# Retention on one core: the query-state product cut into four 64 by 64 quarters, with every second head pair swapped

## The chip, the cores and the metric

The kernel runs on one core of a Trainium2 chip. The metric is the device time of one launch in microseconds. The core has a matrix engine (PE; its weight loads are listed apart as PEld), a vector engine (DVE), a scalar engine (ACT), GpSimd (POOL) and a queue engine (SP) that issues most DMAs. Engines run their own instruction streams in order and meet at semaphores.

## The reference, cut to what matters

```python
scores = scale * np.matmul(q, k.transpose(0, 1, 3, 2))          # B=8, H=8, S=576, D=64
gamma  = 1.0 - 2.0 ** (-5.0 - np.arange(H))
Dmat   = np.where(rel >= 0, gamma[:, None, None] ** rel, 0.0)   # rel = pos_i - pos_j
x      = np.matmul(scores * Dmat, v)                            # retention, (B*S, H*D) = 4608 x 512
logits = x @ w_gate + modality_bias[modality_id]                # 8 experts, one per token
x      = gate * (relu(x @ w1[e]) @ w2[e])                       # routed expert layer
out    = relu(x @ w_in) ** 2 @ w_out                            # dense layer, d_ff = 2048
```

The change touches the first step only, and of the second the product that yields the gate's logits.

## The kernel before, in words

The 4608 tokens go through three stages in one program: `phase0` (retention and routing), `phase12` (expert layers, and a conversion of the dense weights that runs beside them) and `phase3` (the dense layer). The program is written out in a fixed order, and each engine keeps it.

`phase0` works through 36 tiles t of 128 tokens. Since 576 tokens are four and a half tiles, a batch row starts at t % 9 = 0 and another in the middle of t % 9 = 4. The 512 channels are four chunks c of 128 partitions; a chunk holds two heads, head 2c on partitions 0 to 63 and head 2c+1 on 64 to 127. Retention is written as a recurrence: besides the scores inside the tile, a 64 by 64 state for each head (the sum over earlier tiles of key times decayed value) is multiplied with the tile's queries. Per round the program issues, in this order:

- `qk(t+1)`: line 488, scores of the next tile, 8 matmuls with 64 rows by 128 columns of weights, two heads at a time on the two halves of the array's rows, into PSUM banks 0 and 1; line 481 on POOL makes the decayed values `vh`; line 491 on DVE masks the scores into `at`.
- `om(t)`: line 508, the query-state product, 4 matmuls of 128 by 128, one for each chunk. Their weights are the tile `sbd`, in which a chunk's two 64 by 64 states stand on the diagonal of a 128 by 128 block; the other two quarters were set to zero at the start (lines 579 and 580) and stay so. Line 512 adds the scores times `vh`, 8 matmuls with 128 rows by 64 columns, even heads on the left half of the columns, odd heads on the right. All of it goes into bank 2. Line 517 on DVE multiplies it by the decay `odec` into `xt` (lines 520 and 521 where a batch row ends inside the tile). There is no state at t % 9 = 0, and at t % 9 = 4 it counts for 64 of the 128 tokens.
- `kv(t)`: line 536, the state's update in bank 3, and line 542 on ACT, two copies of 64 partitions into the other `sbd`.
- `xm(t-1)`: line 555, `xt` of the tile before times `iwg`, a matrix of the identity (which turns the tile round so that tokens are on partitions) and 8 columns of `w_gate`. The two results go to the banks 5, 6 and 7 in turn; lines 557 and 558 on ACT copy them out.

Routing (`route_a`, `route_b`, `route_c`) is cut into small steps, mostly on DVE, that `adv` sows among these rounds for each group of four tiles: softmax terms, a scaling of four tiles on ACT (lines 193 to 201), a store on SP (line 202), then two small bf16 matmuls (lines 209 and 210) whose result takes the next of the banks 5 to 7, and at last the table of tokens (line 246). The last group is done in one go, and its counts set which expert is gathered first: POOL reads the table (line 431) and issues the gathers (line 434).

Loads are issued on SP, a few at the start on ACT's queue. The program has eight semaphores for them, taken in turn; a DMA's issue waits until the DMA eight before it has landed.

Of the kernel before, what the change touches and what calls it, by code (L numbers as in the profile page):

```python
# [9 lines left out]
F32 = mybir.dt.float32  # L10
# [4 lines left out]
AF = mybir.ActivationFunctionType  # L15
ALU = mybir.AluOpType
# [4 lines left out]
B, H, S, D = 8, 8, 576, 64  # L21
NT, DM = B * S, H * D
NE, FE = 8, 1024
FF = 2048
P = 128
# [5 lines left out]
KD = DM // P  # L31
LC = P + NE
# [11 lines left out]
def consts():  # L44
    gamma = 1.0 - 2.0 ** (-5.0 - np.arange(H, dtype=np.float64))
    scale = 1.0 / np.sqrt(float(D))
    tok = np.arange(9 * P)
    pos = (tok % S).astype(np.float64)
    vdec = scale * gamma[None, :] ** (-(pos[:, None] + 1.0))
    vdec = vdec.reshape(9, P, H).transpose(1, 0, 2)  # L50
    p = np.arange(S, dtype=np.float64)
    od = gamma[:, None] ** (p[None, :] + 1.0)
    odec = np.repeat(od.reshape(KD, 2, 1, S), D, axis=2)
    odec = odec.reshape(KD, P, S).transpose(1, 0, 2)
    j = np.arange(P)
    causal = (j[:, None] <= j[None, :]).astype(np.float64)
    half = causal * ((j[:, None] < 64) == (j[None, :] < 64))
    ident = np.eye(P)
    tri = (j[:, None] < j[None, :]).astype(np.float64)
    ones = np.ones((P, P))  # L60
    m = np.concatenate([causal, half, ident, tri, ones], axis=1)
    rows = {}
    rows["iota"] = np.arange(KEYS, dtype=np.float64)
    rows["rev"] = 8.0 - np.arange(NE)
    rows["k512"] = 512.0 * np.arange(9)
    e = np.arange(NE)
    rows["le"] = (e[None, :] <= e[:, None]).astype(np.float64).reshape(-1)
    rows["eid"] = e
    rows["e36"] = DMAX * e
    s = np.arange(NS)  # L70
    rows["sv"] = np.where(s <= NF, s, s - 1)
    off, cat, o = {}, [], 0
    for k_, a in rows.items():
        off[k_] = (o, len(a))
        o += len(a)
        cat.append(a)
    r = np.repeat(np.concatenate(cat)[None, :], P, axis=0)
    ids = P * np.arange(NTILE)[None, :] + j[:, None] - IDOFF
    off["ids"] = (o, NTILE)
    r = np.concatenate([r, ids], axis=1)  # L80
    f = lambda a: np.ascontiguousarray(a, dtype=np.float32)
    return f(vdec), f(odec), f(m), f(r), off
# [6 lines left out]
def kernel(ctx, tc, qT, kT, kN, vN, modT, w_gate, mbias, w1, w2, w_in, w_out,  # L89
# [28 lines left out]

    psY = Banks(y0=[0], y1=[1], y2=[2], y3=[3], tps=[4])
    psG = Banks(g=[5, 6, 7])  # L120

    xd = dram.tile([NT, DM], F32, name="xd")
    yd = dram.tile([DM, NT + TS], F32, name="yd")
# [5 lines left out]
    ident = const.tile([P, P], F32, name="ident")  # L129
# [22 lines left out]
    G = 4  # L152
# [52 lines left out]
    def route_b(g, eng):  # L205
        t0 = G * g
        oh, pm = OH[g]
        ps = psG.tile([P, G, NE], F32, tag="g", name="psr")
        pe.matmul(ps, trib[:, 0, :], oh, start=True, stop=False, skip_group_check=True)
        pe.matmul(ps, trib[:, 1, :], acc[:, t0:t0 + G, :], start=False, stop=True, skip_group_check=True)  # L210
        yield
        rm = sm.tile([P, G, NE], F32, tag="rm", name="rm")
        rk = sm.tile([P, G], F32, tag="rk", name="rk")
        dd = sm.tile([P, G], F32, tag="dd", name="dd")
        bb = sm.tile([P, G], F32, tag="bb", name="bb")
        ky = sm.tile([P, G], F32, tag="ky", name="ky")
        dve.tensor_scalar(out=ky, in0=pm, scalar1=-float(DMAX), scalar2=float(NE * DMAX),
                          op0=ALU.mult, op1=ALU.add)
        dve.tensor_tensor(out=rm, in0=ps, in1=oh, op=ALU.mult)
        yield  # L220
        dve.tensor_reduce(out=rk, in_=rm, axis=AX.X, op=ALU.add)
        yield
        dve.tensor_scalar(out=dd, in0=rk, scalar1=-63.5, scalar2=1.0 / P, op0=ALU.add, op1=ALU.mult)
        yield
        dve.tensor_scalar(out=dd, in0=dd, scalar1=MAGIC, scalar2=-MAGIC, op0=ALU.add, op1=ALU.add)
        yield
        dve.tensor_tensor(out=ky, in0=ky, in1=dd, op=ALU.add)
        dve.scalar_tensor_tensor(out=bb, in0=dd, scalar=-float(P), in1=rk, op0=ALU.mult, op1=ALU.add)
        yield
        st = wp.tile([P, G * (P + KEYS)], F32R, tag="w", name="okb")  # L230
        ob = st[:, :G * P].rearrange("p (g b) -> p g b", g=G)
        ok = st[:, G * P:].rearrange("p (g b) -> p g b", g=G)
        ids = row("ids")
        RS[g] = (ob, ok)
        for j in range(G):
            eng.tensor_scalar(out=ob[:, j, :], in0=row("iota")[:, :P], scalar1=bb[:, j:j + 1],
                              scalar2=None, op0=ALU.is_equal)
            eng.tensor_scalar(out=ok[:, j, :], in0=row("iota"), scalar1=ky[:, j:j + 1],
                              scalar2=ids[:, t0 + j:t0 + j + 1], op0=ALU.is_equal, op1=ALU.mult)
            yield  # L240
# [8 lines left out]
        dve.tensor_scalar(out=tab, in0=tps, scalar1=IDOFF, scalar2=None, op0=ALU.add)  # L249

    def count(t, name):
        ps = psG.tile([P, NE], F32, tag="g", name=name)
        pe.matmul(ps, trib[:, 1, :], acc[:, t, :], start=True, stop=True, skip_group_check=True)
        return ps

# [182 lines left out]
    def phase0():  # L438
        with ExitStack() as c0:
# [9 lines left out]
            mb = cp.tile([P, 2, NE], F32, name="mb")  # L449
            modi = cp.tile([P, NTILE, 2], I32, name="modi")  # L450
            modf = cp.tile([P, 2, NTILE], F32, name="modf")
            sbd = [cp.tile([P, KD, P], F32, name=f"sbd{i}") for i in range(2)]
            sps = psY.tile([P, KD, D], F32, tag="y3", name="sps")

            U = {}
# [42 lines left out]
            def om(t):  # L498
                b_, a, vn, kn = U[t // 4]
                x = t % 4  # L500
                at, vh = AT[t], VH[t]
                ps = psY.tile([P, KD, P], F32, tag="y2", name="pso")
                tt = t % 9
                ns = 0 if tt == 0 else (64 if tt == 4 else P)
                sb = sbd[scur[0]]
                for c in range(KD):
                    if ns:
                        pe.matmul(ps[:, c, :ns], sb[:, c, :], a[:, c, x * P:x * P + ns],
                                  start=(c == 0), stop=False, skip_group_check=True)
                for c in range(KD):  # L510
                    for i in range(2):
                        pe.matmul(ps[64 * i:64 * i + 64, c, :], vh[:, 2 * c + i, :], at[:, KD * i + c, :],
                                  start=(c == 0 and not ns), stop=(c == KD - 1), skip_group_check=True)
                xt = wk.tile([P, KD, P], F32, tag="xt", name="xt")
                p0 = (t * P) % S
                if p0 + P <= S:
                    dve.tensor_tensor(out=xt, in0=ps, in1=odec[:, :, p0:p0 + P], op=ALU.mult)
                else:
                    n = S - p0
                    dve.tensor_tensor(out=xt[:, :, :n], in0=ps[:, :, :n], in1=odec[:, :, p0:S], op=ALU.mult)  # L520
                    dve.tensor_tensor(out=xt[:, :, n:], in0=ps[:, :, n:], in1=odec[:, :, 0:P - n], op=ALU.mult)
                XT[t] = xt

            def kv(t):
# [11 lines left out]
                        pe.matmul(sps[64 * i:64 * i + 64, c, :], kn[r0:, x, h * D:h * D + D], vh[r0:, h, :],  # L536
                                  start=(new and c == 0), stop=True, skip_group_check=True)
                scur[0] ^= 1
                sb = sbd[scur[0]]
                for i in range(2):  # L540
                    o = 64 * i
                    act.activation(sb[o:o + 64, :, o:o + 64], sps[o:o + 64, :, :], AF.Copy)

            def xm(t):
                g, j = t // G, t % G
# [3 lines left out]
                xt = XT.pop(t)  # L549
                xs = XS[g][:, j, :].rearrange("p (c d) -> p c d", c=KD)  # L550
                for a in range(2):
                    ps = psG.tile([P, 2, LC], F32, tag="g", name="psx")
                    for i in range(2):
                        c = 2 * a + i
                        pe.matmul(ps[:, i, :], xt[:, c, :], iwg[:, c, :], start=True, stop=True,
                                  skip_group_check=True)
                    act.activation(LP[g][:, j, 2 * a:2 * a + 2, :], ps[:, :, P:], AF.Copy)
                    act.activation(xs[:, 2 * a:2 * a + 2, :], ps[:, :, :P], AF.Copy)
# [7 lines left out]
            load(0, 0, 1, both, (2, 3))  # L566
            sp.dma_start(odec[:, :, 0:P], odec_d[:, :, 0:P])
            act.dma_start(ident, mats_d[:, 2 * P:3 * P])
            act.dma_start(iwg[:, :, P:], w_gate.rearrange("(c p) e -> p c e", p=P))
            load(0, 1, 1, both, (2, 3))  # L570
            load(0, 2, 2, parts=(0, 1))
            sp.dma_start(odec[:, :, P:256], odec_d[:, :, P:256])
# [3 lines left out]
            sp.dma_start(modi, modT.bitcast(I32).rearrange("p (t w) -> p t w", w=2))  # L576
            sp.dma_start(mb, mbias.unsqueeze(0).to_broadcast([P, 2, NE]))
            sp.dma_start(trio, mats_d[:, 3 * P:5 * P].rearrange("p (a b) -> p a b", a=2))
            dve.memset(sbd[0], 0.0)
            dve.memset(sbd[1], 0.0)  # L580
            dve.memset(acc[:, 0, :], 0.0)
            noadv = lambda n: None
            qk(0, noadv)
            for c in range(KD):
                pool.tensor_copy(iwg[:, c, :P], ident)
            alloc(1)
            load(1, 4, 4)

# [73 lines left out]
                        stage[t + 4] = lambda g=g: (adv(99), route_c(g))  # L662

    def phase12():
        with ExitStack() as c1:
            xp = c1.enter_context(tc.tile_pool(name="xp", bufs=2))
            hp = c1.enter_context(tc.tile_pool(name="hp", bufs=3))
# [693 lines left out]
```

## Time and profile before

| | |
|---|---|
| Three runs | 1436.12, 1429.42, 1434.08 us; median 1434.08 |
| Profiled execution | 1428.05 us, of which the span from first to last instruction is 1426.3 us |
| Busy over the span | PE 1358.7 us (95%), PEld 1251.9, DVE 1026.4 (72%), ACT 635.8 (45%), POOL 172.6 (12%) |
| `phase0` | 0 to about 194.6 us |
| Mean granted PE clock | 0.984 of full speed |

In a timeline a line is one or more like instructions in a row: start, length, engine, line, tiles, shape and count, and in brackets the idle time before it with what ended it. Each fp32 matmul of the program shows as two records, so the 4 matmuls of line 508 read x8 and the 8 of line 512 read x16. The length of a line of matmuls includes the tail of the last, so what a step costs is read from its start to the start of the next. Shapes of matmuls are given as rows by columns of the array.

### The profile page before, as it was taken

The page shows a single profiled execution, that of the slowest core. Times are in us where ns is not written, and L with a number is a line of the kernel's source. Part 1 is how long each engine was busy: PE and PEld are TensorE (multiplying, and loading weights), DVE is VectorE, ACT ScalarE, POOL GpSimd, SP SyncE. Part 2 cuts the span into 40 slices and gives each one's busy share as a digit, 9 for nine tenths or more (in the row PEclk, how much of TensorE's full clock was granted, in tenths as well). Part 3 has the DMA queues.
Part 4 walks back from the last instruction along what each step waited for, and adds up shares of the span by engine and source line. Part 5 has one row for each costly group of instructions (what it writes and reads, how often), then busy time and mean ns, then how long its engine had stood idle before and what let it go on. Part 6 is the DMA issues. An engine that isn't in the chain of part 4 may idle for free. (4 is left out here: it accounts for less than half of the span.)

```text
span 1426.3 us, 26456 instructions
## 1 busy us (share of the span) xinstructions
PE 1358.7 (95%) x10384; PEld 1251.9 (88%) x10384; DVE 1026.4 (72%) x2004; ACT 635.8 (45%) x1317; POOL 172.6 (12%) x164
## 2 busy tenths in 40 slices
PE   6999998999999999988899999999999999999985
PEld 6898877888788888878899999999999999999984
DVE  2677756887878878553888887767766777688764
ACT  1444543545354454443555555554434444334321
POOL 3222112101110110000211111100000000021112
PEclk9999999999999999998999999999999999999998
DMA  9978256888889888888644455477445564787672
GB/s 341 355 271 296 78 167 229 246 237 254 298 244 269 251 318 229 236 235 272 234 178 178 185 215 194 179 312 265 174 163 195 211 224 184 276 278 274 222 252 102
DMA packets 143733, 332.40 MB, mean 233 GB/s; under 512 B 20208, under 2 KB 54512, under 8 KB 143600
## 3 DMA queue, kind: packets, MB, share of 16 engines
q1 hardware_dynamic: 135520, 310.06, 64.9%
q0 software_dynamic: 5920, 19.40, 3.6%
q8 instruction: 83, 1.36, 0.4%
q10 hardware_dynamic: 2160, 1.17, 0.3%
q14 instruction: 50, 0.41, 0.1%
HBM read 222.57 MB, written 108.02 MB: 232 GB/s over the span
## 5 line engine op out<-in xcount | busy, mean ns | idle before, releaser
L1140 PE MATMUL bank<-w,h 128*128 128x256 f32 x1008 | 284.8, 283 | 9.4 <-DVE h L1241 9.4
L1138 PE MATMUL bank<-w,h 128*128 128x256 f32 x1008 | 283.9, 282 | 7.8 <-DVE oe L1116 7.7
L1138 PE MATMUL bank<-x,w 128*128 128x256 f32 x1008 | 285.8, 284 | 1.4 <-DVE z L1116 0.9
L1139 PE MATMUL bank<-x,w 128*128 128x256 f32 x1008 | 285.7, 283 | 1.5 <-DVE x L1116 1.5
L1140 PE MATMUL bank<-x,w 128*128 128x256 f32 x1008 | 285.4, 283 | 0.1
L1139 PE MATMUL bank<-w,h 128*128 128x256 f32 x1008 | 283.3, 281 | 1.2 <-DMA w<-wc 1.2
L1113 ACT ACTIVATE z<-bank 128x256 f32<-128x256 f32 x288 | 109.1, 380 | 277.2 <-PE bank L1140 258.4
L1140 PEld LDWEIGHTS bank<-w,h 128*128 128x128 f32 x1008 | 190.3, 189 | 12.2 <-DVE h L1241 11.9
L1138 PEld LDWEIGHTS bank<-w,h 128*128 128x128 f32 x1008 | 191.0, 189 | 9.3 <-DVE oe L1116 8.2
L1139 PEld LDWEIGHTS bank<-x,w 128*128 128x128 f32 x1008 | 193.1, 192 | 2.1 <-DVE x L1116 2.1
L1138 PEld LDWEIGHTS bank<-x,w 128*128 128x128 f32 x1008 | 192.7, 191 | 1.8 <-DVE z L1116 1.1
L1140 PEld LDWEIGHTS bank<-x,w 128*128 128x128 f32 x1008 | 193.2, 192 | 0.4 <-DMA w<-wc 0.4
L1139 PEld LDWEIGHTS bank<-w,h 128*128 128x128 f32 x1008 | 190.3, 189 | 1.4 <-DMA w<-wc 1.4
L1240 ACT ACTIVATE h<-z 128x512 fp32r<-128x512 f32 (+2 forms) x270 | 158.1, 599 | 68.4 <-DVE z L1116 46.5
L1241 DVE TENSOR_TENSOR h<-z,h 128x512 fp32r<-128x512 f32 (+2 forms) x270 | 173.8, 672 | 3.7 <-ACT h L1240 3.7
L1116 DVE TENSOR_TENSOR z<-z,bank 128x256 f32<-128x256 f32 x216 | 89.7, 418 | 58.8 <-PE bank L1140 53.4
L787 PE MATMUL bank<-hh,wy 128*128 128x512 f32 (+1 forms) x320 | 127.0, 397 | 5.0 <-ACT hh L803 5.0
L787 PE MATMUL bank<-xh,wx 128*128 128x512 f32 (+1 forms) x320 | 124.5, 389 | 3.4 <-PEq L904 3.4
L788 PE MATMUL bank<-xl,wx 128*128 128x512 f32 (+1 forms) x320 | 124.3, 388 | 1.1 <-DVE xl L743 1.1
L788 PE MATMUL bank<-hl,wy 128*128 128x512 f32 (+1 forms) x320 | 124.4, 389 | 0.7 <-DVE hl L804 0.7
L1116 DVE TENSOR_TENSOR z<-z 128x256 f32<-128x256 f32 x288 | 121.8, 451 | 3.1
L789 PE MATMUL bank<-xh,wx 128*128 128x512 f32 (+1 forms) x320 | 123.9, 387 | 0.0
(168 smaller groups left out, 2223.4 us busy)
## 6 DMA issues: line engine op xcount, KB each, us to landing
x<-xc SPq DMA_DIRECT2D x112, 512.0 KB
wr<-w SPq DMA_DIRECT2D x80, 512.0 KB
xc<-x SPq DMA_DIRECT2D x63, 512.0 KB
w<-wc SPq DMA_DIRECT2D x32, 896.0 KB
wc<-cwh SPq DMA_DIRECT2D x16, 896.0 KB
wc<-cwl SPq DMA_DIRECT2D x16, 896.0 KB
pd<-oe SPq DMA_DIRECT2D x24, 512.0 KB
xd<-xs SPq DMA_DIRECT2D x9, 1024.0 KB
```

Source lines behind the costliest of these rows:

```text
L787: pe.matmul(ps, lh, rh, start=first, stop=False)
L788: pe.matmul(ps, lh, rl, start=False, stop=False)
L789: pe.matmul(ps, ll, rh, start=False, stop=last)
L1113: plan.add(a_(c), lambda e: e.activation(o, i, f), r, w)
L1116: plan.add(engs or d_(c), lambda e: e.tensor_tensor(out=o, in0=a, in1=b, op=op), r, w)
L1138: e.matmul(ps[n], lh, rh, start=first and n == 0, stop=False, skip_group_check=True)
L1139: e.matmul(ps[n], lh, rl, start=False, stop=False, skip_group_check=True)
L1140: e.matmul(ps[n], ll, rh, start=False, stop=True, skip_group_check=True)
L1240: plan.add(a_(c), lambda e: e.activation(h[:, 0, a:b], z[:, a + 1:b + 1], AF.Copy), rs, ks[0])
L1241: plan.add(d_(c), lambda e: e.tensor_tensor(out=h[:, 1, a:b], in0=z[:, a + 1:b + 1], in1=h[:, 0, a:b].bitcast(F32), op=ALU.subtract), rs + ...
```

## The change

The state is kept without zeros: `sbs` holds 64 columns for each chunk. The product is 4 matmuls of 64 by 64 for each pair of chunks, each on another quarter of the array. To let the four of them stand on four quarters, the odd chunks change sides: their even head's result goes to partitions 64 to 127, their odd head's to 0 to 63. Even chunks go into bank 2, odd ones into bank 5. So `odec`, the identity and `w_gate` are laid out with swapped halves for odd chunks, the decay is multiplied bank by bank (two DVE instructions where there was one), the state's copy is one ACT instruction of 128 partitions, and `xm` and the routing in `phase0` have two banks, 6 and 7, where they had three.

```diff
-    odec = np.repeat(od.reshape(KD, 2, 1, S), D, axis=2)
+    od = od.reshape(KD, 2, 1, S)
+    od[1::2] = od[1::2, ::-1].copy()
+    odec = np.repeat(od, D, axis=2)
...
     psG = Banks(g=[5, 6, 7])
+    psX = Banks(g=[6, 7])
+    ring = [psX]
...
-        ps = psG.tile([P, G, NE], F32, tag="g", name="psr")
+        ps = ring[0].tile([P, G, NE], F32, tag="g", name="psr")
...
-            sbd = [cp.tile([P, KD, P], F32, name=f"sbd{i}") for i in range(2)]
+            sbs = [cp.tile([P, KD, D], F32, name=f"sbs{i}") for i in range(2)]
...
-                ps = psY.tile([P, KD, P], F32, tag="y2", name="pso")
+                pso = [banks[i][:, :2 * P].rearrange("p (c t) -> p c t", c=2) for i in (2, 5)]
...
-                sb = sbd[scur[0]]
+                sb = sbs[scur[0]]
+                for a2 in range(0, KD if ns else 0, 2):
+                    for c, i in ((a2, 0), (a2 + 1, 1), (a2 + 1, 0), (a2, 1)):
+                        o = 64 * (i ^ (c & 1))
+                        pe.matmul(pso[c & 1][o:o + 64, c // 2, :ns], sb[64 * i:64 * i + 64, c, :],
+                                  a[64 * i:64 * i + 64, c, x * P:x * P + ns], start=(a2 == 0), stop=False,
+                                  skip_group_check=True)
                 for c in range(KD):
-                    if ns:
-                        pe.matmul(ps[:, c, :ns], sb[:, c, :], a[:, c, x * P:x * P + ns],
-                                  start=(c == 0), stop=False, skip_group_check=True)
-                for c in range(KD):
-                    for i in range(2):
-                        pe.matmul(ps[64 * i:64 * i + 64, c, :], vh[:, 2 * c + i, :], at[:, KD * i + c, :],
-                                  start=(c == 0 and not ns), stop=(c == KD - 1), skip_group_check=True)
+                    for o in (0, 64):
+                        i = (o // 64) ^ (c & 1)
+                        pe.matmul(pso[c & 1][o:o + 64, c // 2, :], vh[:, 2 * c + i, :], at[:, KD * i + c, :],
+                                  start=(c < 2 and not ns), stop=(c >= 2), skip_group_check=True)
...
+                for b in range(2):
+                    od = odec[:, b::2, :]
+                    dve.tensor_tensor(out=xv[:, b, :, :n], in0=pso[b][:, :, :n], in1=od[:, :, p0:p0 + n],
+                                      op=ALU.mult)
...
-                for i in range(2):
-                    o = 64 * i
-                    act.activation(sb[o:o + 64, :, o:o + 64], sps[o:o + 64, :, :], AF.Copy)
+                act.activation(sbs[scur[0]], sps, AF.Copy)
...
-            act.dma_start(iwg[:, :, P:], w_gate.rearrange("(c p) e -> p c e", p=P))
+            for i in range(2):
+                wgs = w_gate.rearrange("(c b p) e -> p c b e", b=2, p=64)
+                for b in range(2):
+                    act.dma_start(iwg[64 * i:64 * i + 64, b::2, P:], wgs[:, b::2, i ^ b])
```

How the order of instructions moves is shown at three places. The first is PE in a plain round, from the product to the state's update, as it was; bank_86 is PSUM bank 2, bank_87 bank 3, and `64x128` is columns of weights by columns that stream.

```order
L508 MATMUL bank_86<-q,sbd_124 128x128 [waits DVE_49,Activation_49]
L508 MATMUL bank_86<-q,sbd_124 128x128 x3
L512 MATMUL bank_86<-at,vh 64x128 [waits Pool_49]
L512 MATMUL bank_86<-at,vh 64x128 x7
L536 MATMUL bank_87<-vh,kn 64x64 x8
```

The same place now; bank_89 is PSUM bank 5, line 513 is the product and line 519 what line 512 was.

```order
L513 MATMUL bank_86<-q,sbs_124 64x128 [waits DVE_49,Activation_49]
L513 MATMUL bank_89<-q,sbs_124 64x128 [waits DVE_49]
L513 MATMUL bank_89<-q,sbs_124 64x128
L513 MATMUL bank_86<-q,sbs_124 64x128 x2
L513 MATMUL bank_89<-q,sbs_124 64x128 x2
L513 MATMUL bank_86<-q,sbs_124 64x128
L519 MATMUL bank_86<-at,vh 64x128 [waits Pool_49]
L519 MATMUL bank_86<-at,vh 64x128
L519 MATMUL bank_89<-at,vh 64x128 x2
L519 MATMUL bank_86<-at,vh 64x128 x2
L519 MATMUL bank_89<-at,vh 64x128 x2
L546 MATMUL bank_87<-vh,kn 64x64 x8
```

Four matmuls have become eight, and the wait on DVE for the bank's release is there twice.

The second place is ACT's queue at the start of the program, before; DMAHW and a number is the DMA semaphore that is waited for.

```order
L568 DMA ident<-mats 128x128 [waits DMAHW1_49]
L569 DMA iwg<-w_gate 128x4x8 [waits DMAHW2_49]
L471 DMA kn<-kN 128x512 [waits DMAHW4_49]
L542 ACT_TABLE_LOAD [waits DVE_49]
L542 ACTIVATE sbd_125<-bank_87 64x4x64 [waits PE_49]
```

And now:

```order
L575 DMA ident<-mats 128x128 [waits DMAHW1_49]
L579 DMA iwg<-w_gate 64x2x8 [waits DMAHW2_49]
L579 DMA iwg<-w_gate 64x2x8 [waits DMAHW4_49]
L579 DMA iwg<-w_gate 64x2x8 [waits DMAHW5_49]
L579 DMA iwg<-w_gate 64x2x8 [waits DMAHW7_49]
L475 DMA kn<-kN 128x512 [waits DMAHW0_49]
L549 ACT_TABLE_LOAD
L549 ACTIVATE sbs_125<-bank_87 128x256 [waits PE_49]
```

One DMA has become four, and the second `kn` load stands behind them, on another semaphore; those of SP's loads shift likewise.

The third place is PE where the routing's small matmuls come, before; bank_89 to bank_91 are PSUM banks 5 to 7, and eight rows of line 488 are left out.

```order
L555 MATMUL bank_90<-iwg,xt 128x136 x2
L555 MATMUL bank_91<-iwg,xt 128x136 [waits Activation_49]
...
L209 MATMUL bank_89<-oh,trib 128x32 [waits Activation_49]
L210 LDWEIGHTS trib
L210 MATMUL bank_89<-acc,trib 128x32 [waits DVE_49]
L508 MATMUL bank_86<-q,sbd_125 128x128 [waits DVE_49,Activation_49]
```

And now:

```order
L562 MATMUL bank_90<-iwg,xt 128x136 [waits Activation_49]
L562 MATMUL bank_90<-iwg,xt 128x136
L562 MATMUL bank_91<-iwg,xt 128x136 [waits Activation_49]
...
L213 MATMUL bank_90<-oh,trib 128x32 [waits Activation_49]
L214 LDWEIGHTS trib
L214 MATMUL bank_90<-acc,trib 128x32 [waits DVE_49]
L513 MATMUL bank_86<-q,sbs_125 64x128 [waits DVE_49]
```

The small matmuls took a bank that nobody had used for a round; now they take the one that `xm` filled just before, and wait for ACT to empty it.

## Rows read from the trace of the kernel before

**Rows 1.** Busy time by stretch: span, PE, PEld, DVE, ACT, POOL (counts), clock, DMA
```profile
0.00:34.80 34.80, 24.05 (x256) 21.79 (x256) 10.47 (x19) 6.06 (x19) 10.74 (x19) 0.90 1.01 340
34.80:165.40 130.60, 130.01 (x1712) 117.48 (x1711) 91.38 (x272) 59.93 (x195) 28.36 (x28) 1.00 0.74 264
165.40:194.60 29.20, 25.79 (x294) 22.82 (x295) 20.42 (x68) 12.32 (x38) 6.39 (x7) 0.94 0.45 158
```

**Rows 2.** PE's timeline, 117 to 126 us: start us, length us, instruction
```profile
117.53 1.16 PE L508 MATMUL bank<-q,sbd 128*128 128x128 f32 x8
118.61 1.09 PE L512 MATMUL bank<-at,vh 128*64 128x128 f32 x16
119.54 0.63 PE L536 MATMUL bank<-vh,kn 128*64 128x64 f32 x16
120.10 1.19 PE L555 MATMUL bank<-iwg,xt 128*128 128x136 f32 x8
121.23 1.16 PE L488 MATMUL bank<-q,k 64*128 64x128 f32 x16
122.32 1.10 PE L508 MATMUL bank<-q,sbd 128*128 128x64 f32 x8
123.35 1.09 PE L512 MATMUL bank<-at,vh 128*64 128x128 f32 x16
124.38 0.68 PE L536 MATMUL bank<-vh,kn 64*64 64x64 f32 x16
124.99 1.19 PE L555 MATMUL bank<-iwg,xt 128*128 128x136 f32 x8
```

**Rows 3.** Groups of like instructions, 34.8 to 165.4 us: busy us, mean ns | idle before
```profile
L508 PE MATMUL bank<-q,sbd 128*128 128x128 f32 x168 | 24.2, 287 | 0.6 <-ACT sbd L542 0.3 <-DVE gg L182 0.2
...
L542 ACT ACTIVATE sbd<-bank 64x256 f32<-64x256 f32 x48 | 18.0, 375 | 35.3 <-PE bank L536 34.8
L517 DVE TENSOR_TENSOR xt<-bank,odec 128x512 f32<-128x512 f32 x24 | 16.5, 688 | 2.0 <-PE bank L512 2.0
```

**Rows 4.** PE's timeline at the start
```profile
22.93 1.19 PE L555 MATMUL bank<-iwg,xt 128*128 128x136 f32 x8
27.54 2.08 PE L488 MATMUL bank<-q,k 64*128 64x128 f32 x16 [3.42 <-DMA q<-qT]
```

**Rows 5.** Timeline of all engines, 165 to 191 us
```profile
165.41 0.69 DVE L491 TENSOR_TENSOR at<-bank,mask 128x512 f32<-128x512 f32 x1 [1.97 <-PE bank L488]
...
171.09 0.36 DVE L168 TENSOR_REDUCE lg<-lp 128x32 f32<-128x128 f32 x1
...
173.36 0.19 PE L209 MATMUL bank<-oh,trib 128*128 128x32 bf16 x1
...
188.98 1.05 POOL L481 TENSOR_TENSOR vh<-v,vdec 128x512 f32<-128x512 f32 x1
190.08 1.57 PEld L512 LDWEIGHTS bank<-at,vh 128*64 128x64 f32 x16 [2.15 <-POOL vh L481]
```

**Rows 6.** Timeline of DVE, a tile in which a batch row ends
```profile
38.07 0.42 DVE L520 TENSOR_TENSOR xt<-bank,odec 128x256 f32<-128x256 f32 x1 [0.79 <-PE bank L512]
38.41 0.41 DVE L521 TENSOR_TENSOR xt<-bank,odec 128x256 f32<-128x256 f32 x1
```

**Rows 7.** Timeline of ACT and PE in a round of the routing
```profile
125.77 0.76 ACT L542 ACTIVATE sbd<-bank 64x256 f32<-64x256 f32 x2
...
126.64 0.38 ACT L558 ACTIVATE xs<-bank 128x256 f32<-128x256 f32 x1
...
127.21 0.19 PE L209 MATMUL bank<-oh,trib 128*128 128x32 bf16 x1
```

**Rows 8.** Timeline of the queues and POOL at the start
```profile
5.75 0.39 ACTq L569 DMA_DIRECT2D iwg<-w_gate  x1
...
7.12 0.33 ACTq L471 DMA_DIRECT2D kn<-kN  x1
...
8.47 0.37 SPq L471 DMA_DIRECT2D q<-qT  x1
...
9.83 0.99 POOL L585 COPY iwg<-ident 128x128 f32<-128x128 f32 x4 [0.20 <-DMA ident<-mats]
```

More of the change, by code (lines that the diff above doesn't have):

```diff
@@ L251, in count @@
     def count(t, name):
-        ps = psG.tile([P, NE], F32, tag="g", name=name)
+        ps = ring[0].tile([P, NE], F32, tag="g", name=name)
         pe.matmul(ps, trib[:, 1, :], acc[:, t, :], start=True, stop=True, skip_group_check=True)
@@ L514, in om @@
+                for c in range(KD):
+                    for o in (0, 64):
+                        i = (o // 64) ^ (c & 1)
+                        pe.matmul(pso[c & 1][o:o + 64, c // 2, :], vh[:, 2 * c + i, :], at[:, KD * i + c, :],
+                                  start=(c < 2 and not ns), stop=(c >= 2), skip_group_check=True)
                 xt = wk.tile([P, KD, P], F32, tag="xt", name="xt")
+                xv = xt.rearrange("p (c b) t -> p b c t", b=2)
                 p0 = (t * P) % S
[L516 to L521, printed above, removed]
+                n = min(P, S - p0)
@@ L522, in om @@
+                for b in range(2):
+                    od = odec[:, b::2, :]
+                    dve.tensor_tensor(out=xv[:, b, :, :n], in0=pso[b][:, :, :n], in1=od[:, :, p0:p0 + n],
+                                      op=ALU.mult)
+                    if n < P:
+                        dve.tensor_tensor(out=xv[:, b, :, n:], in0=pso[b][:, :, n:], in1=od[:, :, 0:P - n],
+                                          op=ALU.mult)
                 XT[t] = xt
@@ L538, in kv @@
                 scur[0] ^= 1
-                sb = sbd[scur[0]]
-                for i in range(2):
-                    o = 64 * i
-                    act.activation(sb[o:o + 64, :, o:o + 64], sps[o:o + 64, :, :], AF.Copy)
+                act.activation(sbs[scur[0]], sps, AF.Copy)
             def xm(t):
@@ L551, in xm @@
                 for a in range(2):
-                    ps = psG.tile([P, 2, LC], F32, tag="g", name="psx")
+                    ps = psX.tile([P, 2, LC], F32, tag="g", name="psx")
                     for i in range(2):
@@ L578, in phase0 @@
             sp.dma_start(trio, mats_d[:, 3 * P:5 * P].rearrange("p (a b) -> p a b", a=2))
-            dve.memset(sbd[0], 0.0)
-            dve.memset(sbd[1], 0.0)
             dve.memset(acc[:, 0, :], 0.0)
@@ L584, in phase0 @@
             for c in range(KD):
-                pool.tensor_copy(iwg[:, c, :P], ident)
+                if c % 2 == 0:
+                    pool.tensor_copy(iwg[:, c, :P], ident)
+                else:
+                    pool.tensor_copy(iwg[:, c, :64], ident[:, 64:])
+                    pool.tensor_copy(iwg[:, c, 64:P], ident[:, :64])
             alloc(1)
@@ L664, in phase12 @@
     def phase12():
+        ring[0] = psG
         with ExitStack() as c1:
```

## The prediction

> **What bounds the kernel now.** I read the busy times by stretch first. PE is busy 130.0 of 130.6 us from 34.8 to 165.4 us, while DVE has 91.4 us of work there, ACT 59.9 and the DMA engines a share of 0.74 [rows 1]: in this stretch, most of `phase0`, what PE saves should be saved by the program. Ahead of it and behind it PE is busy 24.1 of 34.8 and 25.8 of 29.2 us, so there something else ends last. PE's own timeline comes next, because records of matmuls overlap and a step's cost is from start to start. In a plain round the query-state product takes 1.08 us (117.53 to 118.61), the scores times values 0.93, the state's update 0.56, `xm` 1.13 and the next scores 1.09 [rows 2]: 4.79 us, with no gap.
>
> The start is bound by loads: PE ends `xm` at about 24.1 and waits 3.42 us for q, until 27.54 [rows 4]; the DMA engines' share is 1.01 there [rows 1]. The end is bound by chains on other engines: from 165.41, when DVE's wait of 1.97 us for PE is over, DVE works without a pause through the last decay, the last token tables and the softmax that begins at 171.09 and lets PE go on at 173.36; later PE waits 2.15 us for `vh`, which POOL makes only at 188.98, behind its gathers [rows 5].
>
> **Which tiles count.** 32 of the 36 tiles have a state product (not tiles 0, 9, 18, 27). Tiles 1 and 2 lie ahead of the wait at 27.54: nothing. Tiles 31 to 35 lie behind 165.4, under the chains of DVE and POOL: nothing. That leaves tiles 3 to 30 without three, 25 tiles: 24 in the stretch where PE bounds (168 records of 128 columns are 21 tiles [rows 3], and tiles 4, 13 and 22 have 64 columns) and tile 3 before it. Tile 3 runs on the lower of PE's two levels (the scores ahead of it take 2.08 us [rows 4] against 1.16 [rows 2]); I count it as if at the full one.
>
> **The product.** It was 8 records of the whole array, 0.135 us each; it is 16 records of a quarter each. The trace has no such four at once, so the nearest rows bound it:
> - Scores: 16 records on half the rows take 1.09, a pair 0.136, as much as one whole-array record. So two row halves run side by side.
> - Scores times values: 16 records on half the columns, 128 streaming columns, 0.93, a pair 0.116. So column halves run side by side too, and 64 columns of weights cost less than 128.
> - State's update: the same with 64 streaming columns, 0.56, or 0.035 a record; in the form with quarters (lower row half only), 0.61 [rows 2].
>
> If four quarters go at the pair's pace, the product takes 4 x 0.116 = 0.47 us. If only two go at a time, 0.93. No row shows 16 records in less than 0.56; I take that, nearer to the lower end since both kinds of pairs are shown. The tiles with 64 columns have the update's quarters as nearest row: 0.61 for 1.03 before. Saved: 22 x (1.08 - 0.56) = 11.4, and 3 x (1.03 - 0.61) = 1.3: 12.7 us.
>
> A record of 64 columns and 64 rows shows two quarters of the same rows at 0.076 a pair, where one record of the whole array with 64 streaming columns takes 1.03/8 = 0.129 [rows 2]. The Trainium skill, "TensorE: Matmul & The Clock Gate", Part 3, The mechanism, says that a weight load goes beside running matmuls only if its row group differs; by that the third quarter would wait for the first, two would run at a time, and the saving would be that of the first rival below. The row speaks against it without excluding it. The same section's model for packed tiles, one matmul's time and about 4 ns for each further tile, would give by estimate 4 x (0.116 + 0.012) = 0.51 us a product, close to my value.
>
> **Decay on DVE.** One instruction of 0.69 us [rows 3] becomes two of half the size; such a pair takes 0.34 to the second's start and 0.41 for it, 0.75 [rows 6]. 24 x 0.06 = 1.4 us more on DVE, whose load becomes 92.8 of some 118 us: hidden by PE. It is not hidden behind 165.4, where DVE is the chain: tiles 31 (four pieces), 32 and 33 are in it. Bounds: nothing, and 0.06 twice with 4 x 0.42 for 0.75 in tile 31, 1.1 us; I take 0.3.
>
> **State's copy on ACT.** Two instructions of 0.375 take 0.76 [rows 3, 7], one of twice the elements on all partitions about 0.38, as the copies of 256 elements on line 558 take [rows 7]. It ends 0.38 us earlier, but PE waited for it only 0.3 us in all in the stretch [rows 3]. I take nothing; bounds nothing and 0.3 gained.
>
> **Two banks for `xm` and routing.** In the seven routing rounds of the stretch the small matmul now needs the bank that `xm` has just filled. ACT empties it at 126.64 + 0.38 = 127.02, PE gets there at 127.21 [rows 7]. PE will come about 0.45 earlier relative to this chain (the product is in it), ACT 0.38 earlier by the shorter copy: they meet within 0.1. Queued behind the waiting matmul is all of PE. Bounds: nothing, and 7 x 0.4 = 2.8 if ACT's shorter copy gave nothing; I take 0.3.
>
> **Start.** Three more DMA issues on ACT push the second `kn` load back, from 7.12 on, and the q load on SP now waits for the identity's semaphore, not for the one that freed it at 8.47; the identity landed at about 9.83 [rows 8]. So q for tiles 2 and 3 may come 1.4 us later. Tiles 1 and 2 have that slack ahead of 27.54; what counts is the q that PE waits for then, and the engines are full, so the bytes ahead of it decide. Bounds: 1.4 lost, and, if the new order brings that q ahead, the 3.42 us of the wait gained; I take 0.5 lost. POOL's two more identity copies, 0.25 us each [rows 8], fall under the same wait; with no cover they cost 0.5.
>
> **Sum.** 12.7 - 0.3 - 0.3 - 0.5 = 11.6 us. The profiled execution took 1428.05 us (span 1426.3), so 1416.4 for such a one. The median of the runs is 1434.08, 0.4% above; I apply the saving to it: 1422.5 us. The stages behind `phase0` start earlier by the same amount and keep their own pace.
>
> **Rivals.**
> - Two quarters at a time, 0.93 us a product. For: no row shows four, and two streams into one column half share its outlet. Against: the scores already put two row halves into the same columns at full pace. Saved 22 x 0.15 + 3 x 0.10 = 3.6, less 1.1: 1431.6 us.
> - PE gets no longer the bound in the routing rounds: DVE's steps there, with the halved decay, fall behind a round that is 11% shorter. For: DVE is at 70% on average, more in these rounds. Against: PE lost 0.6 us in all to anyone there [rows 3]. Half of the saving goes: 1428 us.
> - Slower: quarters do not overlap at all. Place: line 513; price: 16 x 0.116 = 1.86 for 1.08, and 16 x 0.076 = 1.22 for 1.03: 22 x 0.78 + 3 x 0.19 = 17.7, and 1.1: 1452.9 us. It decides from 0.065 us a record, where 16 records cost 1.04 us and the 1.1 us of side costs eat the rest. Against: both kinds of pairs overlap in the trace.
> - That the product is not cut as said is out: the order of the changed program has eight matmuls of 64 columns in place of four of 128.
>
> **How the numbers follow.** Forecast 67%, two at a time 16%, DVE 10%, no overlap 7%. 0.5% of the time is 7.2 us, about what a measurement can tell from no change. The forecast's own range, with products of 0.47 to 0.65 us and the bounds of the side costs, is 1418 to 1427, all beyond 7.2 us. The DVE case lies at 6, three times in ten beyond. So faster 0.70, same 0.23, slower 0.07. The range: low end 11.6 + 25 x 0.09 + 1.1 = 15 us saved, 1419, and 3 lower because three runs lie 6.7 us apart: 1416; high end the two-at-a-time case, 1432. Only the last rival is outside.
>
> **What would show it.** Right: PE's timeline has the product at about 0.56 us from start to start, 16 records, rounds of about 4.27 us; PE still has no idle time to speak of between about 35 and 153 us; the wait for q at the start grows by about a microsecond, the wait for `vh` at the end likewise. Wrong: a product near 0.93 or 1.9 us; PE waiting for ACT ahead of line 213 in each routing round; PE waiting for DVE ahead of lines 492 or 513; the first long wait ending later than 28.9 us.

## The result, and the profile after

The changed kernel takes 1419.05 us (median of 15 runs, 1415.10 to 1426.43), the kernel before in the same runs 1434.05. The ratio is 0.9917, with a 95% interval of 0.9897 to 0.9936: 9.2 to 14.8 us less. The medians alone lie 15.0 us apart; the ratio, with its interval, is the better measure. Forecast were 1422.5 us within 1416 to 1432, and a saving of 11.6. The profiled executions, 1428.05 us before and 1417.05 after, differ by 11.0.

The first view is the busy time by stretch, with the columns of [rows 1] (us, PE, PEld, DVE, ACT and POOL busy with counts, clock, DMA share, GB/s).

```profile
0.00:34.80 34.80, 22.29 (x273) 19.84 (x274) 9.99 (x21) 4.37 (x13) 10.14 (x21) 0.90 0.97 327
34.80:155.00 120.20, 119.49 (x1908) 105.67 (x1908) 90.72 (x302) 50.96 (x172) 29.19 (x28) 1.00 0.81 290
155.00:185.20 30.20, 25.65 (x338) 21.43 (x335) 20.83 (x74) 11.44 (x35) 6.28 (x7) 0.89 0.47 166
```

The middle stretch, which ends where the last token tables begin, is some 10 us shorter, and PE is still busy in 119.5 of its 120.2 us: the engine that bounded it bounds it still. DVE's share of it rose from 0.70 to 0.75 and is no limit.

PE's timeline, for a plain tile and one with 64 columns (start, length, instruction), answers to [rows 2]:

```profile
111.64 0.67 PE L513 MATMUL bank<-q,sbs 64*64 64x128 f32 x16
112.24 1.09 PE L519 MATMUL bank<-at,vh 128*64 128x128 f32 x16
113.17 0.64 PE L546 MATMUL bank<-vh,kn 128*64 128x64 f32 x16
113.73 1.19 PE L562 MATMUL bank<-iwg,xt 128*128 128x136 f32 x8
114.85 1.16 PE L492 MATMUL bank<-q,k 64*128 64x128 f32 x16
115.94 0.46 PE L513 MATMUL bank<-q,sbs 64*64 64x64 f32 x16
116.34 1.09 PE L519 MATMUL bank<-at,vh 128*64 128x128 f32 x16
```

From start to start the product takes 0.60 us (111.64 to 112.24) where it took 1.08; with 64 columns 0.40 (115.94 to 116.34) where it took 1.03. The other steps of the round are what they were, and the round is 4.30 us (111.64 to 115.94) for 4.79.

The groups of like instructions from 34.8 to 155 us (busy us, mean ns | idle before) answer to [rows 3]:

```profile
L527 DVE TENSOR_TENSOR xt<-bank,odec 128x256 f32<-128x256 f32 x48 | 17.9, 413 | 0.0
...
L513 PE MATMUL bank<-q,sbs 64*64 64x128 f32 x336 | 14.4, 282 | 0.0
...
L213 PE MATMUL bank<-oh,trib 128*128 128x32 bf16 x6 | 1.1, 185 | 0.7 <-ACT xs L565 0.7
```

The busy time of overlapping records says little of their price: 14.4 us for 336 is 0.69 per 16, against 0.60 from start to start. A new wait stands in the last line: in one of six routing rounds PE waits 0.7 us for ACT to empty a bank of `xm`. Ahead of the product no idle time is shown (0.0, before 0.6 in all), but that is not the whole story, for two of the products are longer than the others:

```profile
62.25 0.90 PE L513 MATMUL bank<-q,sbs 64*64 64x128 f32 x16
63.08 1.09 PE L519 MATMUL bank<-at,vh 128*64 128x128 f32 x16
...
80.31 0.82 PE L513 MATMUL bank<-q,sbs 64*64 64x128 f32 x16
81.06 1.09 PE L519 MATMUL bank<-at,vh 128*64 128x128 f32 x16
```

They take 0.83 and 0.75 us from start to start, 0.38 more in all than two of 0.60. In both tiles DVE ends the last piece of the decay of the tile before only after the product has begun (62.44 and 80.41 us), and the product's second matmul waits for DVE to give bank 5 free. So PE most likely waits here inside the group, where no view shows idle time; that is argued from the times, and no run tests it.

At the start, PE's timeline of the changed kernel against [rows 4]:

```profile
28.70 2.08 PE L492 MATMUL bank<-q,k 64*128 64x128 f32 x16 [4.71 <-DMA q<-qT]
30.71 1.13 PE L513 MATMUL bank<-q,sbs 64*64 64x128 f32 x16
31.77 1.97 PE L519 MATMUL bank<-at,vh 128*64 128x128 f32 x16
33.53 1.07 PE L546 MATMUL bank<-vh,kn 128*64 128x64 f32 x16
34.52 1.31 PE L562 MATMUL bank<-iwg,xt 128*128 128x136 f32 x8
35.76 1.16 PE L492 MATMUL bank<-q,k 64*128 64x128 f32 x16
```

And the same stretch of the kernel before, the rows that follow the last one of [rows 4]:

```profile
29.55 2.07 PE L508 MATMUL bank<-q,sbd 128*128 128x128 f32 x8
31.56 1.73 PE L512 MATMUL bank<-at,vh 128*64 128x128 f32 x16
33.12 0.63 PE L536 MATMUL bank<-vh,kn 128*64 128x64 f32 x16
33.68 1.19 PE L555 MATMUL bank<-iwg,xt 128*128 128x136 f32 x8
34.80 1.16 PE L488 MATMUL bank<-q,k 64*128 64x128 f32 x16
```

q comes 1.16 us later (28.70 for 27.54). Tile 3's product wins 0.95 on the lower level (1.06 for 2.01), but 0.75 of that goes: scores times values take 0.20 more (1.76 for 1.56), the state's update 0.43 more (0.99 for 0.56) and `xm` 0.12 more, since these steps ran on the lower level here (granted clock 0.50 until 34.52), where before PE was back on the upper one by the update (1.00 from 33.12). The next scores start 0.96 us late.

At the end, the timeline of all engines of the changed kernel against [rows 5]:

```profile
155.24 0.46 PE L513 MATMUL bank<-q,sbs 64*64 64x64 f32 x16
...
162.39 0.19 PE L213 MATMUL bank<-oh,trib 128*128 128x32 bf16 x1
...
178.49 1.05 POOL L485 TENSOR_TENSOR vh<-v,vdec 128x512 f32<-128x512 f32 x1
...
179.59 1.97 PE L519 MATMUL bank<-at,vh 128*64 128x128 f32 x16 [2.77 <-POOL vh L485]
...
181.50 3.81 PE L562 MATMUL bank<-iwg,xt 128*128 128x136 f32 x16
185.15 1.91 PE L753 MATMUL bank<-ident,xg 128*128 128x128 f32 x16
```

And PE's timeline of the kernel before at the same place:

```profile
190.08 1.97 PE L512 MATMUL bank<-at,vh 128*64 128x128 f32 x16 [1.96 <-POOL vh L481]
191.98 2.76 PE L555 MATMUL bank<-iwg,xt 128*128 128x136 f32 x16
194.58 1.91 PE L740 MATMUL bank<-ident,xg 128*128 128x128 f32 x16
```

The last `vh` comes 10.5 us earlier (178.49 for 188.98). PE's wait for it grew from 1.96 to 2.77 us, and the 16 records of `xm` behind it take 3.65 us, to the start of the next phase at 185.15; before they took 2.60 (191.98 to 194.58). The granted clock within these `xm` records is 0.52, before 0.74: they ran longer on the lower of the two levels (1.2 and 2.4 GHz). That the longer wait is the reason is not shown. With 2.98 or 2.99 us of idle time in the two waits just ahead of the last tile's product and just behind it the same `xm` took 2.60 us (before), 3.22 (the kernel before with four gate loads) and 3.80 (two copies of the state); the changed kernel had 3.35.

So the time came from the stretch between. From tile 4's product to tile 31's it is 118.38 us (36.86 to 155.24) where it was 129.47 (35.90 to 165.37): 11.1 saved. This number repeats: the three runs below that leave PE's records in this stretch as they are, or only reorder them, have 118.35, 118.35 and 118.64, and the kernel before with four gate loads 129.45. About 1 us is lost ahead of it, 0.7 on the way to the next phase, which starts 9.4 us earlier, and 1.7 comes back later, 1.0 of it in a shorter wait for `hh` (4.0 for 5.0 us). The span is 11.1 us shorter.

### The profile page after: what moved, and what is told of

Same layout as the page of the kernel before. It is cut to its first block, busy times and chain, and to the rows that moved or that the text cites. A ratio compares the mean times of both kernels' runs of the same rounds, so it can differ in the third digit from the quotient of the medians.

```text
span 1415.2 us, 26973 instructions
## 1 busy us (share of the span) xinstructions
PE 1346.4 (95%) x10640; PEld 1236.5 (87%) x10640; DVE 1024.9 (72%) x2042; ACT 624.1 (44%) x1285; POOL 170.5 (12%) x166
```

## Experiments

Theory: each 64 by 64 quarter takes its records beside the other three, so that only the number of records in one quarter counts, and with odd chunks of heads on swapped sides all four quarters work. First rival: two quarters work at a time, and the gain is that of smaller tiles. Second rival: it is the order of the records that counts. Ratios are against the kernel before, in runs of their own.

**No swap.** The changed kernel with every head on its old side: 16 records of 64 by 64, all on the two quarters of the diagonal.

```
-                        o = 64 * (i ^ (c & 1))
+                        o = 64 * i
-                        i = (o // 64) ^ (c & 1)
+                        i = o // 64
```

(with the decay table, the identity and the gate's weights unswapped as well).

> The changed kernel with every chunk's heads on their old sides: the product stays eight 64 by 64 matmuls, but only two of the four quarters (upper left, lower right) are used. Mine (four quarters overlap, and the swap is what makes four of them): two at a time, the product takes about 0.93 us instead of the 0.59 of the changed kernel, 25 x 0.34 = 8 us more than it, ratio to before about 0.997. Rival (what pays is the weights' 64 columns instead of 128, and the swap is of no use): 0.59 us, ratio 0.992 as the changed kernel.

Measured: 0.9985 (0.9949 to 1.002), median 1431.74 us. PE's timeline:

```profile
115.52 1.09 PE L512 MATMUL bank<-q,sbs 64*64 64x128 f32 x16
116.54 1.09 PE L518 MATMUL bank<-at,vh 128*64 128x128 f32 x16
...
120.25 0.68 PE L512 MATMUL bank<-q,sbs 64*64 64x64 f32 x16
120.86 0.33 PE L518 MATMUL bank<-at,vh 128*64 128x128 f32 x2
```

The product takes 1.02 us (1.08 in the kernel before), and 0.61 with 64 columns (1.03), and no gain can be measured; by the trace, from tile 4's product to tile 31's, it is 127.33 us, 2.1 less than before. So leaving out the zero halves is worth little of the 11.1 while only two quarters work, more than half of it in the three tiles with 64 columns; the four quarters are the gain. The product is near the price that the first rival of the prediction had guessed (0.93), but from another placing of the weights.

**Same quarter twice in a row.** The changed kernel, with the records ordered so that two of one quarter follow each other.

```
-                for a2 in range(0, KD if ns else 0, 2):
-                    for c, i in ((a2, 0), (a2 + 1, 1), (a2 + 1, 0), (a2, 1)):
+                for c0, i in ((0, 0), (1, 1), (1, 0), (0, 1)) if ns else ():
+                    for c in (c0, c0 + 2):
...
-                                  a[64 * i:64 * i + 64, c, x * P:x * P + ns], start=(a2 == 0), stop=False,
+                                  a[64 * i:64 * i + 64, c, x * P:x * P + ns], start=(c < 2), stop=False,
```

> The changed kernel with the eight matmuls of the product in another order: each two in a row stand on the same quarter (chunks 0 and 2, then 1 and 3, and so on). Mine: neighbours on one quarter wait for each other, so the product takes between 0.93 us (half the overlap lost) and 1.9 us (all of it), 8 to 32 us more than the changed kernel, ratio to before 0.997 to 1.015. Rival (the order is of no matter, the records are paced one by one by issue or weight load at 0.037 us each): 0.59 us, ratio 0.992.

Measured: 0.9917 (0.9885 to 0.9949), median 1419.75 us. PE's timeline:

```profile
111.12 0.69 PE L513 MATMUL bank<-q,sbs 64*64 64x128 f32 x16
111.74 1.09 PE L519 MATMUL bank<-at,vh 128*64 128x128 f32 x16
...
115.45 0.48 PE L513 MATMUL bank<-q,sbs 64*64 64x64 f32 x16
115.86 1.09 PE L519 MATMUL bank<-at,vh 128*64 128x128 f32 x16
```

0.62 and 0.41 us: 0.02 more than the changed order, far from the 0.93 to 1.9 that I had expected. Which quarter a record's neighbour uses hardly matters.

**Rows first.** The changed kernel with two quarters of the same rows one after the other.

```
-                    for c, i in ((a2, 0), (a2 + 1, 1), (a2 + 1, 0), (a2, 1)):
+                    for c, i in ((a2, 0), (a2 + 1, 0), (a2 + 1, 1), (a2, 1)):
```

> The changed kernel with the four quarters in the order upper left, upper right, lower left, lower right, so that neighbours share their rows. Mine (column halves of the same rows overlap as row halves do): product 0.59 us as in the changed kernel, ratio to before 0.992. Rival (a weight load goes beside a running matmul only on other rows): neighbours on the same rows wait, product 0.8 to 1 us, 5 to 10 us more than the changed kernel, ratio 0.995 to 0.999.

Measured: 0.9927 (0.9894 to 0.996), median 1418.27 us. PE's timeline:

```profile
108.01 0.67 PE L513 MATMUL bank<-q,sbs 64*64 64x128 f32 x16
108.61 1.09 PE L519 MATMUL bank<-at,vh 128*64 128x128 f32 x16
```

0.60 us, as in the changed kernel. The rule of the Trainium skill that the prediction weighed ("TensorE: Matmul & The Clock Gate", Part 3, The mechanism: a weight load goes beside running matmuls only if its row group differs) would have made this order slower than the alternating one; the trace does not show it.

**The product twice.** The changed kernel with the 16 records issued twice, which doubles the products with the state in the output.

```
-                for a2 in range(0, KD if ns else 0, 2):
+                for a2 in (0, 2, 0, 2) if ns else ():
```

> The changed kernel with the product issued twice in each tile, the second time anew over the first. Mine (PE bounds 25 of the 32 tiles with a product, at 0.59 us each): 14.8 us more than the changed kernel, ratio to before about 1.002. Rival (all 32 tiles count, the waits at the start and at the end move along with PE): 18.9 us more, ratio 1.005. Rival (PE does not bound, the gain came from elsewhere): under 7 us more, ratio under 0.997.

Measured: 0.999 (0.9967 to 1.0013), median 1429.35 us. PE's timeline:

```profile
76.64 0.69 PE L513 MATMUL bank<-q,sbs 64*64 64x64 f32 x32
77.26 1.09 PE L519 MATMUL bank<-at,vh 128*64 128x128 f32 x16
...
114.63 1.10 PE L513 MATMUL bank<-q,sbs 64*64 64x128 f32 x32
115.67 1.09 PE L519 MATMUL bank<-at,vh 128*64 128x128 f32 x16
...
119.37 0.91 PE L513 MATMUL bank<-q,sbs 64*64 64x64 f32 x32
120.21 0.98 PE L519 MATMUL bank<-at,vh 128*64 128x128 f32 x14
```

Two facts. The second 16 records add 0.44 us with 128 columns (1.04 for 0.60), so some 0.16 of a single pass lies at the group's edges, and 0.22 with 64 columns (0.62 for 0.40, in two of the three tiles; the third, at 119.37, takes 0.84, as its records pause in the middle: 17 start before 119.7, the next at 119.82, for a reason that the trace does not give). And the ratio moved by 0.0073, 10.5 us. The 25 tiles that the prediction counted would give 10.3 us (22 x 0.44 + 3 x 0.22), all 32 of them 13.2; the intervals of the two ratios leave 6 to 15 us by estimate, so the time alone does not tell them apart. The trace does: from tile 4's product to tile 31's it is 127.87 us, 9.5 more, while from tile 31's product to the next phase it is 27.92, no longer than the 29.91 of the changed kernel, and ahead of tile 3's scores PE still waits 0.40 us for q.

**Gate loads on POOL's queue.** The changed kernel with the four small loads of the gate's weights off ACT's queue.

```
-                    act.dma_start(iwg[64 * i:64 * i + 64, b::2, P:], wgs[:, b::2, i ^ b])
+                    pool.dma_start(iwg[64 * i:64 * i + 64, b::2, P:], wgs[:, b::2, i ^ b])
```

> The changed kernel with the four small loads of the gate's weights issued on POOL's queue instead of ACT's, which takes them out of the eight load semaphores. Mine (the wait for q at the start ended 1.16 us later in the changed kernel, 28.70 for 27.54, because three more loads in the ring push k and q back): the wait ends at 27.5 us or a little before, and 1 us or so less than the changed kernel over all, ratio to before about 0.991. Rival (that wait is set by bytes alone and the 1.16 us are chance): it ends at about 28.7 again.

Measured: 0.992 (0.9889 to 0.9951), median 1417.97 us. PE's timeline at the start:

```profile
27.51 1.38 PE L492 MATMUL bank<-q,k 64*128 64x128 f32 x16 [2.61 <-DMA q<-qT]
...
33.38 1.16 PE L492 MATMUL bank<-q,k 64*128 64x128 f32 x16
```

q is back at 27.51 us, where it was before (27.54). That the four loads push it back is supported by this, and by the other traces: with four loads on ACT's queue q comes at 27.85 to 29.45 us in six executions, with one load there at 27.54 and 27.57 (two banks in the kernel before). That it costs the program a microsecond is not shown, since the ratio is that of the changed kernel within what can be measured. The next scores come at 33.38 here, partly because PE was still on its upper level when the scores began (1.38 us against 2.08; granted clock 1.00 until 28.0, 0.50 from 28.4 to 31.65).

**The kernel before with four gate loads.** The kernel before, with the one load of the gate's weights cut into four on the same queue.

```
-            act.dma_start(iwg[:, :, P:], w_gate.rearrange("(c p) e -> p c e", p=P))
+            for i in range(2):
+                for b in range(2):
+                    act.dma_start(iwg[64 * i:64 * i + 64, b::2, P:],
+                                  w_gate.rearrange("(c h p) e -> p c h e", h=2, p=64)[:, b::2, i])
```

> The kernel before with the gate's weights loaded in four parts on ACT's queue, nothing else. Mine: PE's wait for q ends at about 28.7 us instead of 27.54, the rest of the program moves along by 1.2 us. Rival (the later q is due to something else of the change): 27.5 us.

Measured: 1441.44 us, once. PE's timeline:

```profile
16.63 2.08 PE L488 MATMUL bank<-q,k 64*128 64x128 f32 x16 [4.03 <-DMA q<-qT]
...
28.77 1.16 PE L488 MATMUL bank<-q,k 64*128 64x128 f32 x16
```

An earlier q comes at 16.63 instead of 14.46 us, and PE, late by that, reaches the scores at 28.77 with nothing left to wait for. That the loads delay an earlier q is seen; their price is not: tile 3's product ran on the upper level in this execution (1.08 us from 29.87 to 30.95, for 2.01 before), and the routing round ahead of tile 31 began at 164.04 us, ahead of the kernel before's 165.31. The price stays open.

**Two copies of the state.** The changed kernel with the copy on ACT cut in two again.

```
-                act.activation(sbs[scur[0]], sps, AF.Copy)
+                for i in range(2):
+                    o = 64 * i
+                    act.activation(sbs[scur[0]][o:o + 64], sps[o:o + 64], AF.Copy)
```

> The changed kernel with the state's copy on ACT in two instructions of 64 partitions again. Mine (the routing's small matmul meets ACT within 0.1 us only because the copy became shorter): PE waits for ACT ahead of it in seven rounds, about 0.3 us more in each, 2 us in all from 35 to 155 us. Rival (the two banks have slack): no such wait, the changed kernel's one of 0.69 us apart.

Measured: 1422.39 us, once. The rows of PE's timeline that carry a wait for ACT before a routing round:

```profile
47.44 0.18 PE L213 MATMUL bank<-oh,trib 128*128 128x32 bf16 x1 [0.48 <-ACT xs L567]
...
101.60 0.18 PE L213 MATMUL bank<-oh,trib 128*128 128x32 bf16 x1 [1.24 <-ACT xs L567]
```

Six rounds wait (64.99, 83.45, 119.91 and 155.21 are not shown), 3.2 us in all, against one wait of 0.69 in the changed kernel; I had expected seven and 2 us. From tile 4's product to tile 31's it is 121.30 us, 2.9 more. What the two banks would cost is paid by the shorter copy, as the prediction's paragraph on the banks had it.

**Two banks in the kernel before.** The kernel before with `xm` and the routing on two banks.

```
+    psX = Banks(g=[6, 7])
+    ring = [psX]
-                    ps = psG.tile([P, 2, LC], F32, tag="g", name="psx")
+                    ps = psX.tile([P, 2, LC], F32, tag="g", name="psx")
```

(and `ring[0]` in the routing and the counts).

> The kernel before with the banks 6 and 7 alone for xm and the routing, nothing else. Mine: in the routing rounds ACT has emptied the bank at about 127.02 where PE comes at 127.21, so next to nothing in six of seven rounds, and about 0.1 us in the seventh, where PE waited for the state's copy anyway; at the end of the stage PE waits some 0.6 us for DVE to read the early count, off the chain. Rival (two banks cost PE a wait in every round): 24 x 0.1 us or more.

Measured: 1432.85 us, once. PE's timeline, the one routing round that waits:

```profile
108.20 0.18 PE L211 MATMUL bank<-oh,trib 128*128 128x32 bf16 x1 [0.97 <-ACT xs L560]
```

The same round waits in the changed kernel (0.69 at 102.37) and most in the one with two copies (1.24); the kernel before with its three banks waits 0.35 us there, for the state's copy. In the longer rounds of the old product two banks make no new wait in the other rounds; from tile 4's product to tile 31's they cost 0.5 us (129.97 for 129.47).

## Why the prediction was right

- **Which stretch bounds, and which tiles count:** right. PE has no idle time to speak of between 35 and 155 us, and doubling the product made that stretch 9.5 us longer and the stretch behind it no longer.
- **The product:** right in kind, a little off in size. I took 0.56 and 0.61 us; they are 0.60 and 0.40. For 21 tiles of 128 columns and three of 64 between tile 4 and tile 31 that is 21 x 0.48 + 3 x 0.63 = 12.0 us, where the prediction's durations give 21 x 0.52 + 3 x 0.42 = 12.2. Two errors of opposite sign: no single pass came near its lower bound of 0.47, for the group's edges cost 0.16, and the nearest row for 64 columns was a bad one, since the update's quarters use the lower rows alone, two quarters where the product uses four.
- **Two quarters at a time, or no overlap:** both fell. With all four quarters in use, no order made a product of 128 columns longer than 0.62, but for the two tiles in which PE most likely waits inside it.
- **Tile 3:** counted with 0.52 us saved, but the start as a whole lost 0.96 against the forecast's net of nothing (0.5 lost, 0.52 saved). The delay of q was 1.16, inside the bounds of -3.42 to 1.4, and it came the way that the prediction had it: the load of q on SP is issued at 9.86 us for 8.47. The lower level that lasted longer took most of what the product saved. How long it lasts differs from one execution to the next: tile 4's product starts at 36.86 us here, and at 33.25, 34.04, 34.47 and 36.21 in the other traces with the product on four quarters issued once, against 34.66 to 36.21 with the old one. So this term is not settled by one trace.
- **Two banks in the routing rounds:** 0.3 taken, 0.33 measured. The round at 102.37 waits for ACT and is 0.75 us longer up to its small matmul, but of the 0.52 between the second small matmul and the product, where PE waited for the state's copy before, 0.10 is left.
- **The product behind the small matmuls:** not foreseen. In five other routing rounds it starts 0.10 or 0.11 us behind the second small matmul (120.23 to 120.34) where it started 0.02 or 0.03 behind it (127.25 to 127.27): 0.42 in all. The banks are not the reason: the kernel before with two banks has 0.02 or 0.03 there, and the run without the swap 0.10 or 0.11, so it goes with weights of 64 columns.
- **Decay on DVE:** it takes 1.4 us more as forecast (17.9 for 16.5), but most likely not all of it is hidden while PE bounds: the two long products above lost 0.38. Before, PE waited for DVE ahead of one of them (64.05), which cost 0.29. Behind 155 us the decay is in the chain; the four pieces of tile 31 take 0.88 us (157.34 to 158.22), inside the bounds. From tile 31's product to the small matmul of the last full routing round it is 7.15 us (155.24 to 162.39) for 7.99 before (165.37 to 173.36), so no loss is seen there as a whole.
- **The stretch in sum:** 12.0 less 0.33, 0.42 and 0.38, less 0.13 for one token table (0.76 us for 0.63), and 0.29 for the wait that is gone, is 11.0, where 11.1 were seen.
- **The end:** not foreseen. The longer wait ahead of the last tile is what the prediction expected, but not that `xm` behind it would run 1.05 us longer, on the lower level; as said, one pair of executions does not make this a price of the change. It was given back later by shorter waits. So that the sum of 11.6 met the 11.1 of the spans as a whole owes something to luck: errors of about 1 us on both sides cancel. The 11.1 of the bounded stretch, for which the prediction's terms give 11.9 (12.2 less the 0.3 for the banks), do not rest on that.

## What to carry over

A matmul whose weights are half zeros gains little by leaving out the zeros if its parts sit on the same two quarters as before (1.02 us for 1.08 with 128 columns); place them so that all four quarters get the same number of records (0.60), even if data has to change sides on the way. The two other orders tried cost 0.02 us at most. Price such a group from start to start, as records in its busiest quarter plus an edge, and only for the tiles at which PE has no idle time. Look for waits inside the group too: where it goes into two banks, a wait for the second one may show as a longer group and not as idle time. Don't read a microsecond behind a wait at the start or the end from a single trace.

## What was not expected of the hardware

In these runs a product's time goes by the records in its busiest quarter, and not by how many quarters work. With 128 columns four take 0.60 us and eight 1.02 or 1.04 (on two quarters, and on four): 0.105 to 0.11 us a record and about 0.16 at the edges. With 64 columns four take 0.40 us and eight 0.61 or 0.62 (on two quarters, and on four, leaving out the tile that paused): 0.05 to 0.055 us a record, half as much, and a little more, 0.18 or 0.19, at the edges.

Behind a wait for q the steps that ran on the lower level were not the same from one execution to the next: after 3.42 us (before) the scores, the product and most of scores times values; after 4.71 us (changed) the update too; after 2.61 us (gate loads on POOL's queue) the scores began on the upper level, and their end, the product and scores times values ran on the lower. After 1.57 us (two copies) and 0.93 us (rows first) nothing did: the product took its 0.60 us. A microsecond gained or lost at such a place can't be read from the whole time of one execution.
